# First batch's queries block by block; ten blocks' rows of x written later

## The chip, the cores and the metric

One NeuronCore of a Trainium2 chip runs the whole program. The metric is device time in microseconds. The kernel before takes 322.31 us, the median of 3 runs (322.21 to 324.1).

## What is computed

The reference has two parts. The first is attention without softmax, with a decay in place of it, for 8 batches of 8 heads, 576 positions and 64 channels, all in fp32:

```
scores = (1/8) * q @ k^T
ret    = scores * gamma_h ** (i - j)   where i >= j, else 0
x      = (ret @ v), heads side by side  -> 4608 rows of 512
```

The second sends each row of x to one of 8 experts: `logits = x @ w_gate`, the expert is the arg max, the gate its softmax probability, and `out = gate * (relu(x @ w1[e]) @ w2[e])` with matrices of 512x1024 and 1024x512.

## The kernel before, in words

**First half, about 170 us.** The work is tiled in 40 blocks: 8 batches (b) of 5 blocks (c), four of 128 positions and a rest of 64. Block number i is 5b + c. For each block the kernel loads k and v (256 KB each, in runs of 256 bytes, one for each head and position), scales k by the decay (`scale_k`), transposes it on TensorE (`put_TK`) and copies it out of PSUM on ScalarE (`get_TK`). Queries are scaled for a whole batch (`scale_q`, four pairs p of heads) and transposed (`put_TQ`, or `extra_TQ` through another bank). From batch 1 on, `load_q` gives a partition four neighbouring positions, so q moves in runs of 1 KB. `stage_SC` multiplies keys and queries and VectorE masks the product; `stage_AV` multiplies it with v; `stage_S` adds k^T v to a running state, `stage_se` copies that out, and `stage_IN` adds the state times the queries and copies the block's x, transposed, to SBUF. `stage_xb` casts it, `stage_R` turns it back into rows, and `put_rows` writes the rows to a DRAM buffer `x_rows` (128 KB a block). `stage_L1`, `stage_L2` and `route_batch` find each row's expert.

**Batch 0 before.** Its first 128 queries are a tile of their own (`qc0`, L155, scaled and transposed in `first_TQ`); the other 384 come as two loads in runs of 768 bytes (L161) and are scaled and transposed in four pairs (L854 to L862) ahead of `stage_AV(0)`.

**Order.** The order of work on every engine is written by hand. The loop at L917 does for iteration i: scale of k for block i+3, issue of the loads of k for i+9 and of v for i+7, transposes of i+2, `put_rows`, `stage_S(i+1)`, `stage_R(i-2)`, `stage_AV(i)`, `stage_SC(i+1)`, `stage_IN(i)`. Nearly all plain loads and all writes of rows are issued by SyncE (SP), one after the other, in program order; k and v have 7 buffers each, q two.

**Second half.** From block 34 on, the token lists of the experts are made, GpSimd gathers rows from `x_rows` (`gather`, L762) and TensorE runs the experts, with weights that GpSimd and SP load. The first gathers read the rows of batches 0 to 4 (blocks 0 to 24) and so wait for the writes of these.

TensorE is kept running in the first microseconds by transposes that nobody reads (`keep_busy`).

Of the kernel before, what the change touches and what calls it, by code (L numbers as in the profile page):

```python
# [19 lines left out]
P = 128  # L20
# [19 lines left out]
BA = 5  # L40
DW = DM // 2
# [4 lines left out]
def kernel(  # L46
# [48 lines left out]
    wk4 = p1.enter_context(tc.tile_pool(name="wk4", bufs=7))  # L95
    wk1 = p1.enter_context(tc.tile_pool(name="wk1", bufs=1))
# [68 lines left out]
    load_k(3)  # L165
    load_v(2)
    load_k(4)


# [129 lines left out]

# [11 lines left out]
    def put_TQ(ps, o, b, p):  # L311

        qq = qqs.pop((b, p))
        n, _, _ = spans(b)
        for s_ in range(n):
            for u in range(2):
                r = slice(u * DH, (u + 1) * DH)
                tr(ps[:, u, o + s_:o + n * DH:n], qq[r, s_, :], ident[r, r])
# [6 lines left out]
    def get_TQ(ps, o, b, p):  # L325

        n, _, t0 = spans(b)
        nc.scalar.copy(out=q_tile(b)[:, p, t0:512].rearrange("p (u t) -> p u t", u=2), in_=ps[:, :, o:o + n * DH])  # L328
# [8 lines left out]
    def first_TQ():  # L337

        qq = wk3.tile([P, H, DH], F32, tag="kk")
        nc.vector.tensor_tensor(out=qq[:, :, :], in0=qc0[:, :, :],  # L340
                                in1=qg[:, NCOL, :].unsqueeze(2).to_broadcast([P, H, DH]), op=ALU.mult)
        for p in range(NP):
            for u in range(2):
                r = slice(u * DH, (u + 1) * DH)
                tr(psx[:, u, p * DH:(p + 1) * DH],
                   qq[r, 2 * p:2 * p + 2, :].rearrange("p h d -> p (h d)"), ident[r, r])
        nc.scalar.copy(out=q_tile(0)[:, :, 0:P].rearrange("p a (u t) -> p u a t", u=2),  # L347
                       in_=psx[:, :, 0:256].rearrange("p u (a t) -> p u a t", t=DH))
# [10 lines left out]
    def get_TK(ps, o, i):  # L359
# [4 lines left out]
        kTs[i] = kT  # L364

# [134 lines left out]
    def stage_R(i):  # L500
# [17 lines left out]
        xr = wk4.tile([P, NP * P], BF16, tag="xr", name="xr")  # L518
# [6 lines left out]
        todo_x.append((x_rows[t0:t0 + m, 0:DW], xr[0:m, :].bitcast(F32)))  # L525

    todo_x = []
# [307 lines left out]
    def keep_busy(n):  # L835

        for a in range(n):
            tr(scr[:, a % 4 * P:(a % 4 + 1) * P], ident[:, :], ident[:, :])

# [352 lines left out]
```

## Time and profile before

| what | value |
|---|---|
| median of 3 runs | 322.31 us |
| the profiled execution's own time | 322.77 us |
| its span, first to last instruction | 321.0 us |
| TensorE matmul busy | 306.1 us, 95% |
| TensorE weight load busy | 229.3 us, 71% |
| ScalarE busy | 183.2 us, 57% |
| GpSimd busy | 187.0 us, 58% |
| VectorE busy | 150.4 us, 47% |
| moved by DMA | 71.04 MB, mean 221 GB/s |

A busy TensorE is not TensorE at its peak, since a matmul's end is modelled and overlaps the next one. DMA share is the time that packets took as a share of 16 engines; it can go over 1, as packets of one engine overlap. The rows of the trace are in the section below the change.

### The profile page before, as it was taken

How to read it: one execution, taken by the hardware profiler on the slowest of the kernel's cores; microseconds unless marked ns; L12 is line 12 of the kernel's file. 1: busy time of each engine (PE TensorE's matmuls, PEld its weight loads, DVE VectorE, ACT ScalarE, POOL GpSimd, SP SyncE). 2: the span in 40 equal slices, each digit the busy share in tenths (PEclk: the TensorE clock that was granted, in tenths of full speed). 3: DMA queues.
4: the chain of work that ended last, by engine and by line, in shares of the span. 5: the costliest groups of instructions: out<-in, count | busy, mean ns of one | idle time of the engine just before them, and what ended most of it. 6: DMA issues, size and time to landing. Idle time of an engine off the chain costs nothing. (4 is left out here: it accounts for less than half of the span.)

```text
span 321.0 us, 11816 instructions
## 1 busy us (share of the span) xinstructions
PE 306.1 (95%) x4965; PEld 229.3 (71%) x4965; DVE 150.4 (47%) x441; ACT 183.2 (57%) x371; POOL 187.0 (58%) x235
## 2 busy tenths in 40 slices
PE   6899999999999999899999999999999999999993
PEld 5688889888887887788875555677566665757562
DVE  4533366475574747557588321333333425242122
ACT  3568576786766768577576436444645353554530
POOL 4556665535463562445884577678877868564232
PEclk9999999999999999999999999999999999999999
DMA  8989999899999999984999996988999998973221
GB/s 176 233 186 247 200 231 234 214 235 231 237 247 205 257 227 239 242 201 103 204 202 247 212 251 196 254 312 225 286 270 338 249 286 261 305 272 112 77 99 53
DMA packets 114119, 71.04 MB, mean 221 GB/s; under 512 B 89438, under 2 KB 102238, under 8 KB 114064
## 3 DMA queue, kind: packets, MB, share of 16 engines
q1 hardware_dynamic: 102080, 43.84, 54.3%
q0 software_dynamic: 11456, 26.41, 34.0%
q8 instruction: 39, 0.64, 0.9%
q14 instruction: 16, 0.13, 0.1%
q10 hardware_dynamic: 528, 0.02, 0.1%
HBM read 67.31 MB, written 15.26 MB: 257 GB/s over the span
## 5 line engine op out<-in xcount | busy, mean ns | idle before, releaser
L830 ACT ACTIVATE ht<-pm 128x384 bf16<-128x384 f32 (+1 forms) x96 | 49.7, 518 | 54.0 <-PE pm L64 53.2
L304 POOL TENSOR_TENSOR kk<-kt,kg 128x512 f32<-128x512 f32 x39 | 40.9, 1050 | 57.4 <-PE pss L64 26.9
L64 PE MATMUL pm<-xt,w1b 128*128 128x384 bf16 (+1 forms) x512 | 71.1, 296 | 0.2
L64 PEld LDWEIGHTS <-w1b 128*128 128x128 bf16 x512 | 49.8, 98 | 20.0 <-DVE d L632 0.2
L1055 POOL DMA_INDIRECT out_dram<-ys,tids x40 | 42.9, 1073 | 34.8 <-DVE ys L1052 15.9
L429 DVE TENSOR_TENSOR sc<-pssc,mask 128x512 f32<-128x512 f32 x64 | 41.2, 686 | 24.7 <-PE pssc L64 23.9
L64 PEld LDWEIGHTS <-ht 128*128 128x128 bf16 (+1 forms) x328 | 32.5, 105 | 28.0
L762 POOL DMA_INDIRECT xg<-x_rows,tidg x40 | 42.2, 1054 | 14.5 <-issue 8.5
L64 PE MATMUL pss<-w2b,ht 128*128 128x512 bf16 (+2 forms) x168 | 38.8, 374 | 0.0
L64 PE MATMUL psx<-sc,vt 128*64 128x128 f32 (+1 forms) x640 | 38.2, 265 | 0.1
L294 POOL TENSOR_TENSOR qq<-qt,qg 128x512 f32<-128x512 f32 (+1 forms) x28 | 29.2, 1045 | 14.2 <-DMA qt<-in_q_dram 12.3
L64 PE MATMUL py<-w2b,ht 128*128 128x512 bf16 (+2 forms) x160 | 37.0, 374 | 0.0
L64 PE MATMUL pssc<-qT,kT 64*64 64x128 f32 (+2 forms) x896 | 35.5, 259 | 0.3 <-ACT qT L347 0.3
L1052 DVE TENSOR_SCALAR ys<-py,gsl 128x512 f32<-128x512 f32 (+2 forms) x20 | 14.7, 737 | 39.8 <-PE py L64 39.7
L474 ACT COPY xT<-psx 128x512 f32<-128x512 f32 x32 | 18.8, 586 | 25.4 <-PE psx L64 19.5
L811 ACT COPY xt<-pt 128x512 bf16<-128x512 bf16 (+1 forms) x38 | 21.3, 575 | 20.1 <-PE pt L67 19.5
L362 ACT COPY kT<-pst 128x512 f32<-128x512 f32 x40 | 23.6, 589 | 15.9 <-PE pst L67 14.9
L1052 DVE TENSOR_SCALAR ys<-pss,gsl 128x512 f32<-128x512 f32 (+2 forms) x21 | 15.5, 738 | 35.7 <-PE pss L64 34.6
L64 PEld LDWEIGHTS psx<-sc,vt 128*64 128x64 f32 (+1 forms) x640 | 30.6, 136 | 0.9 <-ACT qT L328 0.4
L64 PEld LDWEIGHTS pssc<-qT,kT 64*64 64x64 f32 (+1 forms) x896 | 28.1, 140 | 3.8 <-issue 0.8
L524 ACT COPY xr<-pssc 128x512 bf16<-128x512 bf16 (+1 forms) x37 | 21.9, 593 | 5.5 <-PE pssc L67 5.3
L64 PE MATMUL pss<-vt,kk 128*64 128x64 f32 x512 | 22.4, 227 | 2.6 <-issue 2.0
(141 smaller groups left out, 409.7 us busy)
## 6 DMA issues: line engine op xcount, KB each, us to landing
st<-in_moe_w_dram SPq DMA_DIRECT2D x20, 512.0 KB, 7.0
kt<-in_k_dram SPq DMA_DIRECT2D x32, 256.0 KB, 5.3
vt<-in_v_dram SPq DMA_DIRECT2D x32, 256.0 KB, 4.7
w1b<-in_moe_w_dram POOLq DMA_DIRECT2D x32, 256.0 KB, 6.0
qt<-in_q_dram SPq DMA_DIRECT2D x14, 512.0 KB, 5.4
x_rows<-xr SPq DMA_DIRECT2D x32, 128.0 KB, 4.2
w2b<-in_moe_w_dram POOLq DMA_DIRECT2D x12, 256.0 KB
kt<-in_q_dram SPq DMA_DIRECT2D x8, 128.0 KB, 5.9
```

What stands on the lines that cost most here:

```text
L64: nc.tensor.matmul(out=out, lhsT=lhsT, rhs=rhs, start=start, stop=stop, skip_group_check=True)
L294: eng.tensor_tensor(out=qq[:, 0:n, :].rearrange("p s (h d) -> p h s d", d=DH), in0=qts[b][:, h0:h0 + 2, 0:n, :], in1=qg[:, o:o + n, h0:h0 ...
L304: eng.tensor_tensor(out=kk[:, :, :], in0=kts.pop(i)[:, :, :], in1=kg[:, blocks[i][1], :].unsqueeze(2).to_broadcast([P, H, DH]), op=ALU.mult)
L362: mark["kT"] = nc.scalar.copy(out=kT[:, :, :].rearrange("p a (u t) -> p u a t", u=2), in_=ps[:, :, o:o + 256].rearrange("p u (a t) -> p u ...
L429: mark["sc"] = nc.vector.tensor_tensor(out=sc[:, j, :, :], in0=pssc[j][:, :].rearrange("p (a i) -> p a i", i=P), in1=mask[:, :].unsqueeze( ...
L474: mark["xT"] = nc.scalar.copy(out=xTs[b][:, c, :].rearrange("p (w t) -> p w t", w=2), in_=psx[:, :, 0:2 * P])
L524: nc.scalar.copy(out=xr_out, in_=ps)
L762: nc.gpsimd.indirect_dma_start(out=xg[0:m, :], out_offset=None, in_=x_rows[0:nr, :], in_offset=bass.IndirectOffsetOnAxis(ap=slots[ph][1][0 ...
L811: nc.scalar.copy(out=xts[(e, ph)][:, :, j * P:j * P + m], in_=pt[:, :, 0:m])
L830: mark["mm"] = nc.scalar.activation(out=ht[:, f0:f0 + per, :], in_=pm[:, :, :], func=AF.Relu)
L1052: nc.vector.tensor_scalar(out=ys[0:m, r], in0=py[0:m, r], scalar1=gsl[0:m, e, slots[ph][2] + j:slots[ph][2] + j + 1], scalar2=None, op0=AL ...
L1055: scatters.append(nc.gpsimd.indirect_dma_start(out=next(outs)[:, :], out_offset=bass.IndirectOffsetOnAxis(ap=slots[ph][0][0:m, e, j:j + 1] ...
```

## The change

Batch 0's queries are loaded as four blocks in the same form as k (256 KB, runs of 256 bytes), between the loads of k and v, scaled by VectorE block by block (`scale_qc`) and transposed with the block's keys (`first_T`). The blocks of batch 0 and the first of batch 1 get an order of their own, and the loop starts at i = 6. In it batch 1's queries are transposed at the end of batch 0, and batch 2's in blocks 2 to 4 of batch 1 and not in 1 to 4. The load of the gate weights `wgn` is issued after the first transposes' copies. Rows of blocks 0 to 9 go to ten buffers of their own (`wkr`, list `later`); from i = 16 on, every second iteration passes one of them to `put_rows`, which issues it in the iteration after. The transposes of `keep_busy` become bf16 matmuls on a zeroed tile.

```diff
+LATE = 10
+    wkr = p1.enter_context(tc.tile_pool(name="wkr", bufs=LATE))
...
-    qc0 = attc.tile([P, H, DH], F32, name="qc0")
-    load_k(0)
-    nc.sync.dma_start(out=qc0[:, :, :], in_=q[0, :, 0:P, :].rearrange("h p d -> p h d"))
-    load_k(1)
-    load_v(0)
+    fill = attc.tile([P, 512], BF16, name="fill")
+    nc.vector.memset(fill[:, :], 0.0)
+
+    def keep_busy(n, w=512):
+
+        for _ in range(n):
+            mm(scr[:, 0:w], fill[:, 0:P], fill[:, 0:w], True, True)
+
     qts[0] = ldq.tile([P, H, NCH, DH], F32, tag="q", name="qt")
-    for g in range(2):
-        hs = slice(g * NP, (g + 1) * NP)
-        nc.sync.dma_start(out=qts[0][:, hs, 0:NCH - 1, :],
-                          in_=q[0, hs, P:NCH * P, :].rearrange("h (p s) d -> p h s d", p=P))
-    load_k(2)
-    load_v(1)
-    load_k(3)
-    load_v(2)
-    load_k(4)
+    wgn = attc.tile([P, NPT, E], F32, name="wgn")
+    for c in range(NCH):
+        load_k(c)
+        nc.sync.dma_start(out=qts[0][:, :, c, :], in_=q[0, :, c * P:(c + 1) * P, :].rearrange("h p d -> p h d"))
+        if c > 0:
+            load_v(c - 1)
+    load_k(NCH)
+    load_v(NCH - 1)
+    load_q(1, 0)
+    load_v(NCH)
+    load_k(NCOL)
+    load_q(1, 1)
+    load_v(NCOL)
+    load_k(NCOL + 1)
+    load_v(NCOL + 1)
...
+    def scale_qc(c, eng=nc.gpsimd):
+        if c >= NCH:
+            return
+        qq = wkp.tile([P, NCH, P], F32, tag="qq")
+        eng.tensor_tensor(out=qq[:, :, :].rearrange("p a (h d) -> p (a h) d", d=DH), in0=qts[0][:, :, c, :],
+                          in1=qg[:, NCOL + c, :].unsqueeze(2).to_broadcast([P, H, DH]), op=ALU.mult)
+        qqs[c] = qq
...
+    def only_TQ(b, p):
+        ps = pair_banks()
+        put_TQ(ps, 0, b, p)
+        get_TQ(ps, 0, b, p)
...
+    def first_T(i, n=0):
+        ps = pair_banks()
+        put_TK(ps, 0, i)
+        if n:
+            get_TK(ps, 0, i)
+            keep_busy(n, 256)
+            ps = psx
+            put_TQc(ps, 0, i)
+            get_TQc(ps, 0, i)
+        else:
+            put_TQc(ps, 256, i)
+            get_TK(ps, 0, i)
+            get_TQc(ps, 256, i)
...
-        xr = wk4.tile([P, NP * P], BF16, tag="xr", name="xr")
+        xr = (wkr if i < LATE else wk4).tile([P, NP * P], BF16, tag="xr", name="xr")
...
-        todo_x.append((x_rows[t0:t0 + m, 0:DW], xr[0:m, :].bitcast(F32)))
+        (later if i < LATE else todo_x).append((x_rows[t0:t0 + m, 0:DW], xr[0:m, :].bitcast(F32)))
...
     scale_k(0, nc.vector)
-    stage_T(0, None, None)
-    keep_busy(2)
-    first_TQ()
     nc.vector.memset(psx[:, :, 256:512], 0.0)
+    scale_qc(0, nc.vector)
     nc.vector.memset(lt[:, P + DH:2 * P], 0.0)
     scale_k(1)
-    keep_busy(2)
+    scale_qc(1, nc.vector)
+    keep_busy(9)
+    first_T(0, 1)
+    nc.scalar.dma_start(out=wgn[:, :, :], in_=moe_w_gate.rearrange("(c p) e -> p c e", p=P))
+    keep_busy(3, 256)
     stage_SC(0)
...
+    load_k(NCOL + 2)
+    load_k(NCOL + 3)
+
+    def ahead(i):
+        load_v(i + 7)
+        load_k(i + 9)
+
+    for i in range(NCH):
+        if i == NCH - 1:
+            scale_q(1, 0)
+            scale_q(1, 1, nc.vector)
+            load_q(2, 1)
+        scale_k(i + 2)
+        scale_qc(i + 2, nc.vector)
+        if i == 1:
+            load_q(2, 0)
+        if i < NCH - 1:
+            first_T(i + 1)
+        else:
+            stage_T(i + 1, None, None)
+        put_rows()
+        stage_S(i)
+        stage_R(i - 2)
+        stage_se()
+        stage_xb(i - 1)
+        stage_AV(i)
+        stage_SC(i + 1)
+        stage_IN(i)
+        ahead(i)
+    only_TQ(1, 0)
+    extra_TQ(1, 1)
...
+    scale_q(1, 2)
+    scale_q(1, 3, nc.vector)
+    scale_k(NCOL + 1)
+    make_gate()
...
+    stage_T(NCOL, 1, 2)
+    todo_q.pop()()
+    extra_TQ(1, 3)
+    stage_SC(NCOL)
+    stage_xb(NCH - 1)
+    ahead(NCH)
...
+    stage_T(NCOL + 1, None, None)
+    put_rows()
+    stage_S(NCOL)
...
+    stage_AV(NCOL)
+    stage_L1(0)
+    stage_SC(NCOL + 1)
+    stage_IN(NCOL)
+    stage_S(NCOL + 1)
+    stage_se()
+    stage_T(NCOL + 2, None, None)
+    ahead(NCOL)
...
-        return [2 * c - 6, 2 * c - 5] if b == 0 and c > 2 else [c - 1] if b > 0 and c > 0 else []
+        return ([c - 2] + [c - 1] * (c == NCH) if c > 1 else []) if b == 1 else [c - 1] if c > 0 else []
...
-    for i, (b, c) in enumerate(blocks):
+    for i, (b, c) in list(enumerate(blocks))[NCOL + 1:]:
...
+        if i > 15 and i % 2 == 0:
+            todo_x.extend(later[:1])
+            del later[:1]
```

## Rows read from the trace of the kernel before

**Rows 1.** Stretches: from:to, its length, busy us of each engine, granted clock, DMA share, GB/s.
```profile
20.00:30.00 10.00, 9.04 (x236) 7.68 (x240) 3.71 (x7) 7.58 (x16) 5.99 (x11) 1.00 0.88 202
...
60.00:80.00 20.00, 19.88 (x530) 17.47 (x525) 12.09 (x38) 14.76 (x32) 9.49 (x10) 1.00 0.92 227
...
180.00:200.00 20.00, 20.00 (x126) 11.20 (x124) 4.14 (x10) 10.51 (x21) 13.52 (x16) 1.00 0.94 220
```

**Rows 2.** Timeline, VectorE: masks of blocks 0, 1, 5, 10 and 15 (start, length).
```profile
8.80 1.29 DVE L429 TENSOR_TENSOR sc<-pssc,mask 128x512 f32<-128x512 f32 x2 [0.53 <-PE pssc L64]
15.05 1.29 DVE L429 TENSOR_TENSOR sc<-pssc,mask 128x512 f32<-128x512 f32 x2 [2.79 <-PE pssc L64]
...
31.36 1.29 DVE L429 TENSOR_TENSOR sc<-pssc,mask 128x512 f32<-128x512 f32 x2 [0.22 <-PE pssc L64]
...
50.82 1.29 DVE L429 TENSOR_TENSOR sc<-pssc,mask 128x512 f32<-128x512 f32 x2 [0.21 <-PE pssc L64]
...
69.78 1.29 DVE L429 TENSOR_TENSOR sc<-pssc,mask 128x512 f32<-128x512 f32 x2 [0.22 <-PE pssc L64]
```

**Rows 3.** Timeline, TensorE: two waits, block 5's scores, pieces of a later block.
```profile
24.47 0.46 PE L67 MATMUL pst<-ident,qq 64*128 64x64 f32 x8 [0.96 <-POOL qq L294]
...
30.17 1.16 PE L64 MATMUL pssc<-qT,kT 64*128 64x128 f32 x16
...
36.83 0.69 PE L64 MATMUL pss<-vt,kk 128*64 128x64 f32 x16 [0.65 <-DMA vt<-in_v_dram]
...
110.30 1.08 PE L64 MATMUL pss<-xT,wgp 128*32 128x128 f32 x32
...
112.75 0.41 PE L67 MATMUL pst<-ident,qq 64*128 64x64 f32 x8
113.09 0.69 PE L64 MATMUL pss<-vt,kk 128*64 128x64 f32 x16
```

**Rows 4.** Stretches of 1 us, columns as in rows 1.
```profile
8.00:9.00 1.00, 1.00 (x26) 0.93 (x24) 0.46 (x3) 0.01 (x1) 0.25 (x1) 1.00 1.09 333
...
12.00:13.00 1.00, 0.83 (x14) 0.58 (x16) 0.26 (x1) 0.64 (x2) 0.94 (x1) 1.00 1.35 217
...
15.00:16.00 1.00, 0.99 (x24) 0.79 (x24) 0.95 (x2) 0.58 (x1) 0.44 (x1) 1.00 1.29 180
```

**Rows 5.** Timeline, scaling of queries: block 0, batch 1's first and second half.
```profile
5.48 0.69 DVE L340 TENSOR_TENSOR qq<-qc,qg 128x512 f32<-128x512 f32 x1 [0.85 <-DMA qc<-in_q_dram]
...
23.36 1.06 POOL L294 TENSOR_TENSOR qq<-qt,qg 128x512 f32<-128x512 f32 x1 [1.20 <-DMA qt<-in_q_dram]
...
26.28 1.06 POOL L294 TENSOR_TENSOR qq<-qt,qg 128x512 f32<-128x512 f32 x1 [0.41 <-DMA qt<-in_q_dram]
```

**Rows 6.** Writes of rows on SP: first, tenth, one late; all 40, issue to landing.
```profile
40.09 1.30 SPq L533 DMA_DIRECT2D x_rows<-xr  x1
...
74.04 0.92 SPq L533 DMA_DIRECT2D x_rows<-xr  x1
...
146.85 0.61 SPq L533 DMA_DIRECT2D x_rows<-xr  x1
...
DMA to landing us min/median/max: 2.3/4.3/13.6
```

**Rows 7.** First gather on GpSimd, its use on TensorE, gathers' time to landing.
```profile
150.83 1.13 POOL L762 DMA_INDIRECT xg<-x_rows,tidg  x1 [0.54 <-DVE tidg L746]
...
160.83 0.40 PE L67 MATMUL pss<-identb,xg 128*128 128x128 bf16 x4
...
DMA to landing us min/median/max: 2.8/5.6/10.6
```

**Rows 8.** TensorE's gaps with no releaser; the queue of instruction fetches.
```profile
128.49 0.50 PE L64 MATMUL pss<-vt,kk 128*64 128x64 f32 x9 [0.60 <-issue]
...
134.23 0.51 PE L64 MATMUL pss<-vt,kk 128*64 128x64 f32 x10 [0.97 <-issue]
...
q8 instruction: 39, 0.64, 0.9%
```

More of the change, by code (lines that the diff above doesn't have):

```diff
@@ L313, in put_TQ @@
         qq = qqs.pop((b, p))
-        n, _, _ = spans(b)
-        for s_ in range(n):
+        for s_ in range(NCH):
             for u in range(2):
                 r = slice(u * DH, (u + 1) * DH)
-                tr(ps[:, u, o + s_:o + n * DH:n], qq[r, s_, :], ident[r, r])
+                tr(ps[:, u, o + s_:o + NCH * DH:NCH], qq[r, s_, :], ident[r, r])
     def q_tile(b):
@@ L344, in first_TQ, with get_TQc @@
                 r = slice(u * DH, (u + 1) * DH)
[L345 to L348, printed above, removed]
+                tr(ps[:, u, o + p * DH:o + (p + 1) * DH], qq[r, p, :], ident[r, r])
+    def get_TQc(ps, o, c):
+        nc.scalar.copy(out=q_tile(0)[:, :, c * P:(c + 1) * P].rearrange("p a (u t) -> p u a t", u=2),
+                       in_=ps[:, :, o:o + 256].rearrange("p u (a t) -> p u a t", t=DH))
     def put_TK(ps, o, i):
@@ L524, in stage_R @@
             nc.scalar.copy(out=xr_out, in_=ps)
-        todo_x.append((x_rows[t0:t0 + m, 0:DW], xr[0:m, :].bitcast(F32)))
-    todo_x = []
+        (later if i < LATE else todo_x).append((x_rows[t0:t0 + m, 0:DW], xr[0:m, :].bitcast(F32)))
+    todo_x, later = [], []
     def put_rows():
@@ L832, in mm1 @@
         return ht
-    def keep_busy(n):
-        for a in range(n):
-            tr(scr[:, a % 4 * P:(a % 4 + 1) * P], ident[:, :], ident[:, :])
-    keep_busy(12)
     scale_k(0, nc.vector)
-    stage_T(0, None, None)
-    keep_busy(2)
-    first_TQ()
     nc.vector.memset(psx[:, :, 256:512], 0.0)
+    scale_qc(0, nc.vector)
     nc.vector.memset(lt[:, P + DH:2 * P], 0.0)
     scale_k(1)
-    keep_busy(2)
-    stage_SC(0)
-    stage_T(1, None, None)
-    stage_S(0)
-    stage_se()
-    keep_busy(3)
@@ L854 @@
-    for p in range(NP):
-        scale_q(0, p, nc.vector if p % 2 else nc.gpsimd)
-    scale_k(2)
-    for p in range(NP):
-        ps = psx if p % 2 == 0 else pair_banks()
-        put_TQ(ps, 0, 0, p)
-        get_TQ(ps, 0, 0, p)
-        if p == 1:
-            keep_busy(2)
-    stage_AV(0)
-    stage_IN(0)
-    stage_SC(1)
-    for i in range(5, 9):
-        load_v(i - 2)
-        load_k(i)
-        if i < 7:
-            load_q(1, i - 5)
+    scale_qc(1, nc.vector)
+    keep_busy(9)
+    first_T(0, 1)
@@ new lines @@
+    only_TQ(1, 0)
+    extra_TQ(1, 1)
+    constants = make_routing()
+    next(constants)
+    scale_q(1, 2)
[3 more added lines that the diff above has]
+    put_rows()
+    stage_S(NCH)
+    stage_R(NCH - 2)
+    stage_IN(NCH)
+    stage_T(NCOL, 1, 2)
[4 more added lines that the diff above has]
+    ahead(NCH)
+    next(constants)
+    scale_k(NCOL + 2)
+    load_q(3, 0)
+    stage_T(NCOL + 1, None, None)
+    put_rows()
+    stage_S(NCOL)
@@ L872, in pairs @@
+    stage_R(NCOL - 2)
+    stage_se()
+    stage_xb(NCH)
+    scale_k(NCOL + 3)
+    stage_AV(NCOL)
[6 more added lines that the diff above has]
+    ahead(NCOL)
     def pairs(b, c):
@@ L923 @@
         scale_k(i + 3)
-        if i == 1:
-            make_gate()
-        if i > 3:
-            next(constants, None)
+        next(constants, None)
         if b == B - 1 and c > 0:
@@ L960 @@
             stage_L2(b - 1)
-        for stage in ((stage_SC, stage_IN) if c < NCH else (stage_IN, stage_SC)) if i > 0 else ():
+        for stage in ((stage_SC, stage_IN) if c < NCH else (stage_IN, stage_SC)):
             stage(i + 1 if stage is stage_SC else i)
```

30 lines of the change are left out of this document (9 added, 21 removed).

## The prediction

> **What bounds the kernel now.** I read the stretches first. From 60 to 80 us TensorE is busy 19.88 of 20 us, from 180 to 200 us all 20; from 20 to 30 us it is busy 9.04 of 10 [rows 1]. So TensorE sets the pace of both halves, and only the start has holes. DMA is not far behind: its share is 0.88 to 0.94 in the same rows.
>
> The masks of VectorE then show the pace batch by batch [rows 2]. From block 10 to block 15, one steady batch, 69.78 - 50.82 = 18.96 us. Batch 1 takes 50.82 - 31.36 = 19.46 us, batch 0 31.36 - 8.80 = 22.56 us, and its first block alone 15.05 - 8.80 = 6.25 us. What can be won is here, before 31 us; batch 1 has 0.5 us over the steady pace, the rest has next to nothing that loads or writes of rows cause.
>
> TensorE's own waits say what the holes are [rows 3]: at 24.47 it has waited 0.96 us for scaled queries of batch 1, and at 36.83 it waits 0.65 us for a load of v (block 7). GpSimd, which scales those queries, waited in turn for their loads, 1.20 us before 23.36 and 0.41 before 26.28 [rows 5]. So the start is set in part by the chain of steps (queries of three blocks transposed in four rounds before block 0's products with v), in part by arrival of loads. SP issues them in program order and DMA moves them one behind the other, so I cost the start by bytes ahead of a load.
>
> **The change part by part.**
>
> *Block 0's path.* Now block 0 needs k0, q0 and v0 and no rounds of the other blocks' queries. But VectorE has `scale_qc(1)` queued ahead of block 0's mask: it waits for q1, the fourth load. In the kernel before, the second load's scaling starts at 5.48 [rows 5]; two more loads of 0.262 MB at 217 GB/s [rows 4] are 1.2 us each, so q1 lands near 7.9 and its 0.69 us end near 8.6, just before 8.80. Bounds 0 and +0.7 us for the mask; I take +0.3, as the early load rate is no better than that row. Block 1's mask then has q2 (0.69 us) ahead of it on VectorE. q2 is the seventh load, five after q0: 5.5 + 5 x 1.2 = 11.5, scaled by 12.2, so the mask comes near 12.8 and not 15.05: 2.2 us gained at that point.
>
> *Queries of batch 0 in runs of 256 bytes.* In the stretch from 8 to 9 us, where the 768-byte loads of batch 0's queries move, DMA gives 333 GB/s; from 12 to 13 us, with only k and v in runs of 256 bytes, 217 at an even higher share, 1.35 against 1.09; from 15 to 16 us 180 [rows 4]. So the three blocks, 0.786 MB, take 3.6 us and not 2.4: +1.3 us for everything behind them (at 180 GB/s +2.0; nothing if only bytes counted). The Trainium skill, "DMA: Bandwidth & Descriptors", section Specifications, wants at least 512 bytes a transfer for line rate, which speaks against this edit; the trace agrees with 333 against 217 GB/s. Were bytes all that counted, the sum below would be 1.3 us better.
>
> *Order of the loads.* The second half of batch 1's queries decides block 5, since its scores need all four pairs. Ahead of it one load of k (k6) is gone: -1.2 us; the runs give +1.3. So it lands where it did, 26.3 [rows 5]. From there: 1.06 us of scaling on GpSimd [rows 5], with k5 scaled before it, in its shadow, then two query transposes of 0.34 us each (113.09 - 112.75) [rows 3] and a copy that the second hides: block 5's scores start at 28.4 and not 30.17 [rows 3], **1.8 us earlier**. TensorE can keep that date: at the steady batch's pace, less 1.08 us for the logits [rows 3] and plus three query transposes of 0.34 us, batch 0 needs 18.9 us, 3.7 less than it took.
>
> Next the load of v for block 7. Before, it landed at 36.83 and TensorE waited for it [rows 3]. The change moves half of batch 2's queries (0.524 MB, at 333 GB/s 1.6 us) and k9 (1.2 us) behind it, against the 1.3 us of the runs: it lands near 35.3. TensorE would want it at 36.83 - 0.65 - 1.8 = 34.4, plus two products and transposes that now stand behind block 5's scores, 0.4 to 0.8 us: near 35. So about 0.3 us goes into a new wait, and the gain is 36.83 - 35.3 = **1.5 us**. The queries that were moved come 2.8 us after, near 38.1, and are scaled by 39.2; TensorE wants them near 38.8, as their transposes moved a block later too: 0 to 0.4 us, which the missing transpose of block 1 (0.34 us) pays.
>
> *Rows written late.* SP issues the first write of rows at 40.09 and the tenth at 74.04 [rows 6], so the loads up to there lose ten writes ahead of them (two are of half blocks). But by then TensorE waits for no load any more (batch 2 is at the steady pace) [rows 2]. The ten writes come back at one in two blocks from about 80 us to the last block row issue near 147. The cover is the loads' lead, and if that is gone each costs its place, 128 KB at 217 GB/s, 0.6 us. I take 0; bounds -0.5 us (batch 1's excess gone) and +1 us.
>
> *The rest, each at nothing.* The bf16 fillers end before k0's transposes are wanted, or stand at most 0.5 us in their way, hidden behind q0 at 5.5 us. The gate weights' load and preparation move to GpSimd's time after k6, and are wanted only by batch 0's logits. The extra 10 buffers of rows lengthen no step. The load of `wgn` waits on ScalarE for nothing that stands behind it.
>
> **The sum.** -1.5 us, from about block 8 to the end, as all that follows is paced by TensorE. Against the profiled execution's 322.77 (span 321.0 and 1.8 around it) that is 321.3; the execution lies 0.46 over the median of 322.31, so against the median **320.8 us**. What a measurement of this kernel can tell from no change is about 1%, 3.2 us: 319.1 to 325.5 is the same.
>
> **The rivals.**
>
> 1. *Loads hold nothing up; TensorE's pace alone sets batch 0.* For it: the sum of bytes is rough, DMA dips in the first 40 us (share 0.88) [rows 1] could be filled by the shorter lists of waits on SP, and without writes the lead grows. Against: [rows 3, 5] show the waits for loads. Then 3.7 us of batch 0 and 0.5 of batch 1 are won, a little more since batch 0 lacks the small routing products: 322.3 - 4.2 = 318.1.
> 2. *Gaps of instruction fetch go as well.* TensorE stands 0.60 and 0.97 us in the middle of a group of matmuls without any releaser, and a queue fetches instructions through the same engines [rows 8]. If a fuller DMA makes these, the lead won before 75 us takes them away: -1.5 - 1.6, 319.2, or 318.5 with part of the waits of rival 1. Against: two gaps in one execution are few.
> 3. *The gain is given back.* If the 256-byte loads run at 180 GB/s [rows 4] from the start, the 3.8 MB in such runs up to the second half of batch 1's queries take 3.6 us longer than at 217, or 1.8 if half of them do; block 5 is then at 30 to 31 and nothing is won: 322.3, up to 323.5.
> 4. *Slower: the first gather waits for a late write.* The last of the ten is issued near 147, like the late write of [rows 6], and the first gather, at 150.83, reads the rows of blocks 0 to 24 and so now waits for it. A gather lands in 5.6 us in the median [rows 7] and TensorE wants it at 160.83, so the write may land as late as 155.2, 8 us after its issue. The median is 4.3, the longest 13.6 [rows 6]. At 13.6 it lands at 160.6, the gather at 166.2, and TensorE stands 5.4 us: 320.8 + 5.4 = 326.2. Behind the gather on GpSimd stand the first experts' weight loads and the next gathers; these have more time. For it: the added wait is real. Against: DMA is at its slackest there, and 8 us are nearly twice the median.
> 5. *The edit does less than it says*, since the tenth write's turn or the order on VectorE undoes it: this falls into 3.
>
> **How the numbers follow.** My forecast, gains of 0.6 to 2.8 us: 0.45. Rival 1: 0.16. Rival 2: 0.10, both over 1% faster or at its edge. Rival 3 (with 5): 0.20. Rival 4: 0.09, most of it just over 1% slower. So faster 0.25, same 0.67, slower 0.08. The range goes from 317.2 (rival 1 with 1 us more for the routing products that batch 0 lacks) to 324.2 (rival 3 with the +1 us of the late writes, short of rival 4); the forecast's own range is 319.5 to 321.7.
>
> **What would show it.** After: block 1's mask near 12.8, block 5's near 29.6 and block 10's near 49.3; a load wait at block 7's state product below 0.7 us; 217 to 250 GB/s from 2 to 20 us with no stretch over 300; writes of rows on SP from about 62 us on (block 10's) and block 0's near 80; the first gather with no wait for a write. Wrong if block 5's mask comes before 28 (loads did not bind) or after 30.5 (they ran slower), if the gain at block 10 is not the gain at the end, or if TensorE waits for the first gathered rows.

## The result

The change makes the kernel slower: 328.23 us median (22 runs, 323.46 to 331.72) against 322.48 us for the kernel before beside it (22 runs), a ratio of 1.0121 [1.009, 1.0152], 3.9 us of 322.48. 320.8 us was forecast, and 324.2 us was the end of the range. The profiled execution took 331.49 us, span 329.7, so it is one of the longer ones. All ratios here are to the kernel before in the same job on the same chip and count undisturbed runs alone (none over 1.5% above the fastest of its kernel), while the medians take in all runs. The kernel before has medians of 322.5 to 330.2 us in the six jobs, over 2% apart, and 324.3, 329.5 and 330.2 us in three jobs on one chip; so the times of different jobs are not set against each other; the traces are, one execution each.

The masks of the changed kernel, the answer to [rows 2] (VectorE timeline; blocks 0, 1, 5, 10 and 15; line numbers are the changed file's, so L454 is the mask that was L429, L65 the matmul that was L64):

```profile
8.28 1.29 DVE L454 TENSOR_TENSOR sc<-pssc,mask 128x512 f32<-128x512 f32 x2
12.13 1.28 DVE L454 TENSOR_TENSOR sc<-pssc,mask 128x512 f32<-128x512 f32 x2
...
32.57 1.29 DVE L454 TENSOR_TENSOR sc<-pssc,mask 128x512 f32<-128x512 f32 x2 [4.41 <-PE pssc L65]
...
55.02 1.29 DVE L454 TENSOR_TENSOR sc<-pssc,mask 128x512 f32<-128x512 f32 x2 [0.26 <-PE pssc L65]
...
76.26 1.29 DVE L454 TENSOR_TENSOR sc<-pssc,mask 128x512 f32<-128x512 f32 x2 [1.48 <-PE pssc L65]
```

Block 1 is 2.9 us earlier than before, block 5 is 1.2 us later, block 10 is 4.2 us later, block 15 6.5. The last masks of the loop begin at 172.47 and 163.83 us, and from there to the end both take 157.2 us. So in these two executions the loss has two places, batch 1 (blocks 5 to 10: 22.45 us, was 19.46) and blocks 10 to 39 (117.45 us, was 113.01); the second half has none.

Stretches of the changed kernel, the answer to [rows 1] (columns as there):

```profile
20.00:30.00 10.00, 7.65 (x193) 6.42 (x186) 4.15 (x7) 5.50 (x12) 5.90 (x8) 0.91 0.92 215
30.00:40.00 10.00, 9.23 (x173) 8.10 (x171) 2.94 (x5) 4.97 (x11) 5.45 (x19) 0.75 0.99 194
60.00:80.00 20.00, 18.68 (x486) 16.29 (x487) 11.93 (x37) 13.62 (x29) 9.24 (x9) 1.00 0.88 197
180.00:200.00 20.00, 20.00 (x131) 11.13 (x130) 8.51 (x31) 10.15 (x21) 11.38 (x17) 1.00 1.17 229
```

From 20 to 30 us TensorE is busy 7.65 of 10 us (9.04 before), and the granted clock is 0.91 there and 0.75 in the next 10 us: it stood at half, the lower of its two levels, from 28.1 to 35.0 us. Before, it was full from 6.7 us to the end of the span's work. From 60 to 80 us TensorE lacks 1.3 us, with DMA slacker than before (197 GB/s, was 227).

What stands ahead of the half clock (TensorE timeline; block 5's key transposes, its queries, its scores; then the key transposes of blocks 7 and 8):

```profile
25.98 0.46 PE L68 MATMUL pst<-ident,kk 64*128 64x64 f32 x8
28.80 0.69 PE L68 MATMUL pst<-ident,qq 64*128 64x64 f32 x8 [2.35 <-POOL qq L294]
29.42 1.11 PE L68 MATMUL scr<-ident,qq 128*128 128x128 f32 x4
30.46 2.08 PE L65 MATMUL pssc<-qT,kT 64*128 64x128 f32 x16
...
38.32 0.46 PE L68 MATMUL pst<-ident,kk 64*128 64x64 f32 x8
39.56 0.47 PE L68 MATMUL pst<-ident,kk 64*128 64x64 f32 x8 [0.77 <-POOL csb L624]
```

and the scalings that TensorE waits for, the answer to [rows 5] (GpSimd and VectorE):

```profile
21.89 1.06 POOL L294 TENSOR_TENSOR qq<-qt,qg 128x512 f32<-128x512 f32 x1 [1.40 <-DMA qt<-in_q_dram]
22.07 1.42 DVE L294 TENSOR_TENSOR qq<-qt,qg 128x512 f32<-128x512 f32 x1
27.13 0.69 DVE L294 TENSOR_TENSOR qq<-qt,qg 128x512 f32<-128x512 f32 x1 [2.83 <-DMA qt<-in_q_dram]
27.15 1.59 POOL L294 TENSOR_TENSOR qq<-qt,qg 128x512 f32<-128x512 f32 x1 [2.25 <-DMA qt<-in_q_dram]
```

From 26.4 us TensorE has nothing that it may start, and it stands 2.35 us. The second half of batch 1's queries lands at 27.1, and both engines start on it at the same moment: GpSimd's scaling, the one that TensorE wants first, takes 1.59 us and not 1.06. Behind the gap the same four transposes of a pair take 1.11 us that take 0.66 at the full clock, and block 5's scores 2.08 (1.16 in [rows 3]). The last row is a wait that the kernel before does not have: the key transposes of blocks 7 and 8 now follow one another directly, and both go to the one pair of PSUM banks (`pst2`, one buffer), which ScalarE must first copy out. (The releaser named there is a wait that ended last by the profile; the run that moves these transposes apart, below, shows the cause.)

The largest stall further on (TensorE timeline, the scores of block 20, the first of batch 4):

```profile
94.28 1.16 PE L65 MATMUL pssc<-qT,kT 64*128 64x128 f32 x14
97.61 0.38 PE L65 MATMUL pssc<-qT,kT 64*128 64x128 f32 x2 [2.17 <-issue]
97.74 0.49 PE L68 MATMUL pst<-ident,kk 64*128 64x64 f32 x8
```

It has no releaser and falls in the middle of a group, like the two gaps of [rows 8]. If all of TensorE's instructions in the trace are counted in their order, such gaps fall where the count passes number 192 of a group of 256. One packet of the instruction queue [rows 8] seems to hold such a group: 39 packets of 16 KB go with 10,011 instructions of TensorE in the changed kernel, one for 257.

"Stalls" below are the steps of over 0.4 us at these marks, from the start of one instruction to the start of the next, added up (so each has the length of one instruction in it, and a few end with a wait that has a releaser). From 7 us to the end of the loop's blocks they come to 7.7 us, in the kernel before to 2.7; those that begin between 50 and 96 us to 5.0 and 0. TensorE's idle time with no releaser at the marks is less, 4.3 and 2.0 us, between 50 and 96 us 3.6 and 0, and the largest of these gaps runs past 96 us.

That these are late fetches shows in all traces together. They have 570 packets of the instruction queue between 7 us and the loop's last mask. Where a packet landed less than 1 us before TensorE came to the next mark, a stall followed in 88 of 93 cases; where it landed earlier, in 18 of 477.

```profile
50.00:96.00 46.00, 45.77 (x1197) 40.00 (x1196) 29.67 (x90) 33.05 (x71) 23.63 (x24) 1.00 0.95 229
```

```profile
50.00:96.00 46.00, 43.02 (x1110) 37.01 (x1100) 27.12 (x86) 31.51 (x67) 20.53 (x20) 1.00 0.95 214
```

The first row is the kernel before, the second the changed one: TensorE loses 2.75 us of this stretch at the full clock, with DMA equally busy; 2.0 us of it are idle time at the marks.

### The profile page after: what moved, and what is told of

Same layout as the page of the kernel before. It is cut to its first block, busy times and chain, and to the rows that moved or that the text cites. A ratio compares the mean times of both kernels' runs of the same rounds, so it can differ in the third digit from the quotient of the medians.

```text
span 329.7 us, 11796 instructions
## 1 busy us (share of the span) xinstructions
PE 309.6 (94%) x4957; PEld 230.2 (70%) x4957; DVE 151.9 (46%) x444; ACT 182.6 (55%) x370; POOL 184.6 (56%) x231
## 5 line engine op out<-in xcount | busy, mean ns | idle before, releaser
L65 PE MATMUL pm<-xt,w1b 128*128 128x384 bf16 (+1 forms) x512 | 71.1, 296 | 0.2
L65 PEld LDWEIGHTS <-w1b 128*128 128x128 bf16 x512 | 49.9, 98 | 20.0 <-DVE d L657 0.2
L454 DVE TENSOR_TENSOR sc<-pssc,mask 128x512 f32<-128x512 f32 x64 | 41.3, 686 | 27.2 <-PE pssc L65 27.0
L65 PEld LDWEIGHTS <-ht 128*128 128x128 bf16 (+1 forms) x328 | 32.5, 105 | 28.3 <-issue 0.4
L787 POOL DMA_INDIRECT xg<-x_rows,tidg x40 | 42.9, 1074 | 14.6 <-issue 7.6
L65 PE MATMUL pssc<-qT,kT 64*64 64x128 f32 (+2 forms) x896 | 37.5, 262 | 3.9 <-issue 3.6
L65 PE MATMUL psx<-sc,vt 128*64 128x128 f32 (+1 forms) x640 | 38.9, 267 | 0.3 <-issue 0.3
L65 PE MATMUL pss<-w2b,ht 128*128 128x512 bf16 (+2 forms) x168 | 38.8, 374 | 0.0
L65 PE MATMUL py<-w2b,ht 128*128 128x512 bf16 (+2 forms) x160 | 36.9, 374 | 0.1
L65 PEld LDWEIGHTS pssc<-qT,kT 64*64 64x64 f32 (+1 forms) x896 | 29.4, 143 | 8.3 <-issue 4.7
L499 ACT COPY xT<-psx 128x512 f32<-128x512 f32 x32 | 18.8, 587 | 26.0 <-PE psx L65 20.0
L836 ACT COPY xt<-pt 128x512 bf16<-128x512 bf16 (+1 forms) x38 | 21.3, 574 | 19.9 <-PE pt L68 19.3
L65 PEld LDWEIGHTS psx<-sc,vt 128*64 128x64 f32 (+1 forms) x640 | 31.3, 137 | 1.0 <-issue 0.4
L294 POOL TENSOR_TENSOR qq<-qt,qg 128x512 f32<-128x512 f32 x25 | 27.0, 1081 | 3.6 <-DMA qt<-in_q_dram 3.6
L65 PE MATMUL pss<-vt,kk 128*64 128x64 f32 x512 | 23.0, 230 | 1.6 <-issue 0.9
```

Source lines behind the costliest of these rows:

```text
L65: nc.tensor.matmul(out=out, lhsT=lhsT, rhs=rhs, start=start, stop=stop, skip_group_check=True)
L294: eng.tensor_tensor(out=qq[:, :, :].rearrange("p s (h d) -> p h s d", d=DH), in0=qts[b][:, h0:h0 + 2, :, :], in1=qg[:, 0:NCH, h0:h0 + 2].r ...
L454: mark["sc"] = nc.vector.tensor_tensor(out=sc[:, j, :, :], in0=pssc[j][:, :].rearrange("p (a i) -> p a i", i=P), in1=mask[:, :].unsqueeze( ...
L499: mark["xT"] = nc.scalar.copy(out=xTs[b][:, c, :].rearrange("p (w t) -> p w t", w=2), in_=psx[:, :, 0:2 * P])
L787: nc.gpsimd.indirect_dma_start(out=xg[0:m, :], out_offset=None, in_=x_rows[0:nr, :], in_offset=bass.IndirectOffsetOnAxis(ap=slots[ph][1][0 ...
L836: nc.scalar.copy(out=xts[(e, ph)][:, :, j * P:j * P + m], in_=pt[:, :, 0:m])
```

## The experiments

The table has nineteen profiles, one execution each: the start of block 5's and of block 10's mask, the time from block 10's to block 39's, the sum of the stalls that begin between 50 and 96 us (all in us), and the ratio of the timed runs to the kernel before. "Held" means that the first ten blocks' rows are written late; so they are in the changed kernel and in all its variants but e1, w1, x3 and z3.

| kernel | block 5 | block 10 | 10 to 39 | stalls | ratio |
|---|---|---|---|---|---|
| before | 31.36 | 50.82 | 113.0 | 0 | |
| before (b0) | 31.70 | 50.47 | 115.6 | 0 | |
| before (z4) | 31.64 | 51.07 | 112.6 | 0 | |
| w2, before, buffers only | 31.27 | 50.59 | 116.6 | 1.2 | 1.0005 [0.9948, 1.0062] |
| e2, before, held | 30.79 | 50.72 | 121.1 | 4.9 | 0.997 [0.9926, 1.0015] |
| y3, before, held, short lead | 31.96 | 53.10 | 116.5 | 3.6 | 1.0126 [1.0017, 1.0236] |
| changed | 32.57 | 55.02 | 117.5 | 5.0 | 1.0121 [1.009, 1.0152] |
| a0, changed again | 30.21 | 51.23 | 116.9 | 4.1 | 1.0101 [1.0035, 1.0166] |
| e3, fillers | 31.88 | 52.89 | 116.8 | 3.0 | 1.0116 [1.0044, 1.0187] |
| x1, rows twice | 32.61 | 56.33 | 118.8 | 4.4 | 1.0176 [1.0096, 1.0257] |
| x2, rows at the end | 31.20 | 53.95 | 118.0 | 4.6 | 1.0107 [1.0021, 1.0192] |
| y1, short lead | 30.32 | 54.58 | 114.5 | 1.3 | 1.0135 [0.9999, 1.0272] |
| y2, queries first | 32.67 | 55.13 | 116.4 | 5.4 | 1.0168 [1.0063, 1.0272] |
| z2, banks apart | 30.61 | 52.10 | 119.5 | 2.7 | 1.0135 [1.0048, 1.0223] |
| e1, rows at once | 31.18 | 55.24 | 112.5 | 0 | 1.0045 [1.0001, 1.009] |
| w1, buffers only | 29.50 | 50.51 | 115.2 | 1.6 | 1.018 [1.012, 1.024] |
| x3, at once, spaced | 29.94 | 56.75 | 117.8 | 4.2 | 1.0071 [1.0022, 1.0119] |
| z1, fewer bytes | 27.10 | 49.62 | 113.4 | 2.6 | 1.0019 [0.9969, 1.007] |
| z3, all mended | 27.12 | 48.77 | 112.5 | 1.7 | 0.9974 [0.9934, 1.0014] |

The first theory (A) was the gap for batch 1's queries and the half clock behind it; its rivals were instruction fetches that come late (B), for which the rows written late might be the reason, through their collisions with other transfers (C) or through their absence from the first 75 us (D), mere chance of single executions (E), and in the end the loads' lead, that is, how many blocks ahead of the masked one they are issued (F).

**a0: the changed kernel again**, unedited, in another job.

> The changed kernel once more, beside the others. Theory A (the clock): the wait of 2.35 us for the second half of batch 1's queries lowers the granted clock for some 7 us, so an execution with a drop after 28 us (mean clock under 0.993) is about 3.4 us longer than one without. Theory B (instruction fetch): TensorE's own instructions arrive later than before (packet of a fetch 3.1 us after the last boundary, 2.3 before), and its gaps at every 256th instruction add some 4 to 5 us; then executions without a clock drop are still 3 to 4 us over the kernel before.

1.0101: the loss is there again. But the gap for the second half of the queries is 0.59 us in the profiled execution, the clock does not fall there, and block 10 is at 51.23. So A cannot be all of it.

**e1: rows written at once** (without the ten buffers too, as `wkr` then has one).

```diff
-LATE = 10
+LATE = 0
```

> The changed kernel with rows of x written as before, none held back. If the late writes make the loss (rival C: they collide with loads and instruction fetches after 80 us), this is 3 to 5 us faster than the changed kernel. If the order of the first batch makes it (A and B), it stays within 1.5 us of the changed kernel, that is 3 to 6 us over the kernel before; if held-back rows did help, it is 1 to 2 us slower than the changed kernel.

**e2: the kernel before with the rows held back alone** (`wkr`, `later` and the two lines of the loop that pass rows on).

> The kernel before with the late rows alone: ten buffers, written one every second block from iteration 16 on. Rival C: 3 to 5 us slower than before. Theories A and B, if the new order of loads and of TensorE's first batch is what matters: within 1.5 us of before (320.5 to 324).

The new start without the held rows is at 1.0045, still not faster; the held rows without the new start are at 0.997, within the noise. Blocks 10 to 39 point the other way: 112.5 us in e1 without a stall between 50 and 96 us, 121.1 in e2.

**e3: fillers over the gap.**

```diff
+    keep_busy(11)
     stage_T(NCOL, 1, 2)
```

> The changed kernel with 11 filler matmuls (2.3 us) ahead of block 5's transposes, where TensorE waited 2.35 us for queries. Theory A: the granted clock stays full from 5 us to the end (mean 0.995 or more in all executions), batch 1 takes 2 to 3 us less, and the median falls by half of 3.4 to all of it, 1.7 to 3.4 us. Theory B alone: the clock stays full but the gaps at the instruction boundaries remain, and the time stays 3 to 4 us over the kernel before.

In the profiled execution the clock stayed full from 4.5 to 171.7 us, and its time lies within the others of this kernel; the ratio is 1.0116 all the same. The timed runs tell only their mean clock (0.990 to 0.996), not where it fell. A alone has fallen as far as one trace can show it.

**b0: the kernel before, a second profile, on the chip of the next runs.**

> The kernel before once more, for a second profile of it. Theory D (held-back rows let the loads run on alone; small reads at full rate delay TensorE's instruction fetches): between 50 and 96 us no gap at an instruction boundary, or under 0.7 us in all, and packets of 256 bytes take 18 to 19 ns in the mean from 50 to 75 us. If gaps there are chance (rival E), this profile has 2 us or more of them as likely as the changed kernel's.

Batch 1 takes 18.77 us there and nothing stalls between 50 and 96 us.

**x1: the missing writes put back** as writes of the same rows to a spare tile at the old time.

```diff
+        if i < LATE:
+            todo_x.append((spare[i * P:i * P + m, 0:DW], xr[0:m, :].bitcast(F32)))
```

> The changed kernel, which also writes the ten blocks' rows to an unused DRAM buffer at the time at which the kernel before writes them: 1.2 MB more traffic, the late writes as they were. Theory D: with writes between the loads again, the gaps at instruction boundaries from 50 to 96 us (2.5 to 5 us in the profiles with held-back rows) fall under 1 us and the time by 1 to 3 us against the changed kernel. Rival C (the late writes collide with loads): no gain, 0 to 1.5 us slower than the changed kernel.

**x2: the held rows all written from block 33 on.**

```diff
-        if i > 15 and i % 2 == 0:
-            todo_x.extend(later[:1])
-            del later[:1]
+        if i == NB - 8:
+            todo_x.extend(later)
+            del later[:]
```

> The changed kernel with all ten held-back rows written together at block 33, when loads are nearly done, and none from 80 to 140 us. Theory D: gaps from 50 to 96 us stay at 2.5 to 5 us and the time within 1.5 us of the changed kernel. Rival C: 1.5 to 3 us faster than it.

Stalls of 4.4 and 4.6 us remain, and the ratios stay at 1.0176 and 1.0107, so neither D (x1) nor C (x2) explains them.

**x3: rows at once, block 7's transposes earlier, batch 2's queries paired as before.**

```diff
+    stage_T(NCOL + 2, None, None)
     stage_IN(NCOL)
     stage_S(NCOL + 1)
     stage_se()
-    stage_T(NCOL + 2, None, None)
...
-        return ([c - 2] + [c - 1] * (c == NCH) if c > 1 else []) if b == 1 else [c - 1] if c > 0 else []
+        return [c - 1] if c > 0 else []
```

> The changed kernel with rows written at once, and two places of its order mended: block 7's transposes ahead of block 6's state, so that they and block 8's no longer follow each other through the one pair of PSUM banks (a gap of 0.8 to 0.9 us near 35 us in all profiles of the new order), and batch 2's queries one pair a block as before (a gap of 0.58 us at block 9). Theory: batch 1 takes 1.1 us less than with the rows-at-once version (21 us without clock drops), and the time is within 1 us of before; if these gaps are covered by later waits, it stays 1.5 us over before.

A mend that did harm: with the old pairing TensorE wants batch 2's queries before they are there, stands 3.75 us ahead of 39.48, and the clock falls to half from 37.6 to 44.4 us.

**y1 and y3: a short lead of the loads**, in the changed kernel and in e2's.

```diff
-        load_k(i + 9, mark.get("sc"))
+        if not 8 <= i <= 10:
+            load_k(i + (9 if i < 8 else 6), mark.get("sc"))
...
-        load_v(i + 7, mark.get("xT"))
+        if not 8 <= i <= 10:
+            load_v(i + (7 if i < 8 else 4), mark.get("xT"))
```

> The changed kernel, but from block 11 on a block's step loads k of six blocks ahead and v of four, not nine and seven (three steps load nothing in between), so that the loads' lead over the masked block stays at about 6, where it was in the kernel before, and not at 8. Theory F (the instruction fetches come late, and TensorE stands at every such place, because the loads run against the limit of their buffers): the sum of TensorE's stalls at the 256-instruction marks between 50 and 96 us falls from 4 to 5 us to below 1.5, the fetches' mean delay there from 3.4 us to about 2, and the run is 2 to 4 us below the changed kernel, ratio to the kernel before 0.998 to 1.005. Rival (the stalls belong to the new load on the engines, or to where the fetches fall, and not to the lead): stalls of 3 to 5 us remain and the ratio stays at 1.008 to 1.013. If the short lead starves the blocks, TensorE shows waits for kt or vt.

> The kernel before with the rows of the first ten blocks held back (as in the run with that part alone) and the lead of the loads kept short as in the run before this one. Theory F: the stalls between 50 and 96 us, 4.9 us with the rows held back alone, fall below 1.5, and the ratio to the kernel before comes to 0.985 to 0.994. Rival: stalls of 4 to 5 us and a ratio of 0.995 to 1.0, as without the cap.

The lead did fall to 5 or 6 blocks. The stalls came to 1.3 us in one and 3.6 in the other, and neither time fell: y3 is at 1.0126, the same kernel with the long lead (e2) at 0.997. F is not shown; at most a part is.

**y2: the second half of batch 1's queries loaded earlier.**

```diff
     load_q(1, 0)
+    load_q(1, 1)
     load_v(NCH)
     load_k(NCOL)
-    load_q(1, 1)
```

> The changed kernel, but the second half of batch 1's queries is loaded right behind the first half, ahead of v of block 4 and k of block 5, 2.4 us earlier. If the load order is what made TensorE stand 2.35 us for those queries, and the half clock from 28 us followed from that gap, then the wait ahead of block 5's scores is below 0.5 us, the clock stays full from 5 to 100 us in the profile, block 5's mask is at 29.5 to 30.5 and the run is 1.5 to 2.5 us below the changed kernel (ratio to the kernel before 1.003 to 1.007). If block 4's v or block 5's keys become the wait in their place, the same gap shows at block 4's product or block 5's transposes and the ratio stays at 1.01.

The one gap became several: 1.30 us at 22.04 and 0.71 at 27.71 for keys, 1.07 at 29.25 for queries, and block 5's mask stays at 32.67. So moving this one load forward gains nothing; what holds block 5 is the sum of the loads ahead of it, or the engines' own work. z1 tells these apart.

**z1: two loads of queries left out.** Blocks 1 and 2 use block 0's queries, so the output is another, and all work of the engines stays.

```diff
     for c in range(NCH):
         load_k(c)
-        nc.sync.dma_start(out=qts[0][:, :, c, :], ...
+        if c == 0:
+            nc.sync.dma_start(out=qts[0][:, :, c, :], ...
...
-        eng.tensor_tensor(..., in0=qts[0][:, :, c, :],
+        eng.tensor_tensor(..., in0=qts[0][:, :, 0, :],
```

> The changed kernel, but the queries of blocks 1 and 2 are not loaded (0.524 MB in runs of 256 bytes less); the queries of block 0 are used in their place, so the numbers are wrong and all the work of the engines stays. If the arrival of loads sets block 5 (the bytes ahead of batch 1's second half of queries), that half comes 2.4 us earlier (0.524 MB at 220 GB/s), the wait ahead of it, 0.6 to 2.35 us in the runs so far, goes, and block 5's mask comes at 28 to 29.5 (29.9 to 32.7 in all nine runs of the new order). If the engines' own work sets it, block 5's mask stays at 30 to 32. And if batch 1's excess is made by the loads too, blocks 5 to 10 fall from 21 to 27 us to about 20; if it is made by the new order of TensorE's work, they stay at 21 or more.

TensorE's timeline of z1 where the changed kernel has its gap:

```profile
24.20 0.46 PE L68 MATMUL pst<-ident,kk 64*128 64x64 f32 x8
24.51 0.41 PE L68 MATMUL pst<-ident,qq 64*128 64x64 f32 x8
24.88 0.66 PE L68 MATMUL scr<-ident,qq 128*128 128x128 f32 x4
25.60 1.47 PE L65 MATMUL pssc<-qT,kT 64*128 64x128 f32 x16
```

No wait: block 5's scores start at 25.60, its mask at 27.10, 2.4 to 5.6 us earlier than in the eleven profiles of the new order with all loads. So the arrival of loads binds block 5, and the ratio comes to 1.0019. (z2, of the same job, has all loads and is at 1.0135; the two intervals just overlap.) Batch 1 still takes 22.5 us, with the bank wait (0.77 us at 33.06) and two gaps at the fetch marks (0.41 and 0.91 us) in it.

**z2: the two transposes through the one pair of banks moved apart.**

```diff
     stage_SC(NCOL + 1)
+    stage_T(NCOL + 2, None, None)
     stage_IN(NCOL)
     stage_S(NCOL + 1)
     stage_se()
-    stage_T(NCOL + 2, None, None)
```

> The changed kernel, but block 7's key transposes stand right behind block 6's scores, ahead of block 5's and block 6's state products, so that they and block 8's no longer follow each other through the one pair of banks. The theory of the bank pair: the wait of 0.77 us, the same in eight profiles, is gone, and blocks 5 to 10 take 0.7 us less than otherwise; in the time that is a ratio about 0.002 lower than the changed kernel's, under what these rounds can tell. If the copy is only late for another reason, the wait moves to another place of the same two blocks.

TensorE's timeline of z2 at that place:

```profile
34.72 0.47 PE L68 MATMUL pst<-ident,kk 64*128 64x64 f32 x8
35.11 0.69 PE L65 MATMUL pss<-vt,kk 128*64 128x64 f32 x16
35.95 0.46 PE L68 MATMUL pst<-ident,kk 64*128 64x64 f32 x8 [0.16 <-ACT kT L373]
36.63 0.69 PE L65 MATMUL pss<-vt,kk 128*64 128x64 f32 x16 [0.21 <-ACT se L431]
```

0.77 us of waiting became 0.16 and 0.21 (ScalarE now has two copies close together): 0.4 us gained, not 0.7. The time cannot show that (1.0135).

**z3: both edits and rows at once.**

> Both edits above, and rows written at once: the new start with neither the late loads, nor the bank wait, nor the rows held back. If these three are what eats the start's 4 us, block 5's mask is at 28 to 29.5, block 10's at 48 to 49.5, the stalls at 256-instruction marks between 50 and 96 us below 1.5 us, and the ratio to the kernel before 0.988 to 0.996. If something else of the new order eats it (stalls of the instruction fetch in the denser start, the half clock behind them), block 10's mask stays at 51 or more and the ratio at 1.0 or above.

Masks of z3, blocks 0, 1, 5, 10 and 15:

```profile
8.69 1.29 DVE L455 TENSOR_TENSOR sc<-pssc,mask 128x512 f32<-128x512 f32 x2 [1.96 <-PE pssc L65]
11.77 1.29 DVE L455 TENSOR_TENSOR sc<-pssc,mask 128x512 f32<-128x512 f32 x2 [1.12 <-PE pssc L65]
...
27.12 1.29 DVE L455 TENSOR_TENSOR sc<-pssc,mask 128x512 f32<-128x512 f32 x2 [1.92 <-PE pssc L65]
...
48.77 1.29 DVE L455 TENSOR_TENSOR sc<-pssc,mask 128x512 f32<-128x512 f32 x2 [0.26 <-PE pssc L65]
...
69.32 1.29 DVE L455 TENSOR_TENSOR sc<-pssc,mask 128x512 f32<-128x512 f32 x2 [1.80 <-PE pssc L65]
```

Block 10 is 2.1 us ahead of the kernel before, and the ratio is 0.9974 [0.9934, 1.0014], against 1.0135 [1.0048, 1.0223] for z2 in the same job. The gain of 0.4 to 1.2% that was expected is not shown: in the trace one stall of 1.7 us takes most of the lead at block 15.

**z4: the kernel before, once more.**

> The kernel before, once more in profile on this chip. If batch 1's length is a property of the order, its blocks 5 to 10 take 18.8 to 19.9 us here too (19.46 and 18.77 in the two profiles so far; 21.0 to 26.8 in nine of the new order). If it is chance of single executions, some 21 us or more can show here as well.

Batch 1 takes 19.43 us. It takes 18.8 to 19.9 us in five of the six profiles of the old order (21.1 in y3) and 21.0 to 26.8 in the eleven of the new order with all loads, so its length is a property of the order.

**w1 and w2: the ten buffers, but rows written at once**, in the new and the old order.

```diff
-        (later if i < LATE else todo_x).append(
+        todo_x.append(
```

> The changed kernel with the ten extra buffers of rows, but each block's rows written at once. Stalls of TensorE at the 256-instruction marks between 50 and 96 us came to 1.3 to 5.4 us in all eleven profiles with rows held back and to 0, 0, 0, 0, 1.7 and 4.2 us in the six with rows written at once. If the lateness of the writes makes them, they fall below 1.7 us here, and the ratio to the kernel before is that of rows at once, 1.00 to 1.009. If it is the ten buffers (another place of all later buffers in SBUF), 2.5 to 5 us stay and the ratio is 1.008 to 1.016.

> The kernel before with the ten extra buffers of rows, rows written at once. Lateness: no stalls between 50 and 96 us (0 in three profiles of the kernel before), ratio 0.995 to 1.005. The buffers: 2.5 to 5 us of stalls, ratio 1.005 to 1.015.

Stalls of 1.6 and 1.2 us: by the traces it is the lateness more than the buffers. The times don't follow: w1 is at 1.018 [1.012, 1.024], no better than with rows held and worse than e1 (1.0045 [1.0001, 1.009]), which differs from it by the ten buffers alone but ran in another job. In the old order the same buffers cost nothing that shows (w2, 1.0005). So the times leave the buffers open as a cause.

No version here is shown to beat the kernel before; z3 leaves out loads that the kernel needs.

## Why the prediction was wrong

**Block 0's path: right.** Block 0's mask came at 8.28 (9.1 forecast), block 1's at 12.13 (12.8), and blocks 1 to 3 stay 2 to 3 us ahead.

**Runs of 256 bytes: borne out, but not tested alone.** Stretch from 2 to 20 us, before and after, and two short ones after:

```profile
2.00:20.00 18.00, 16.52 (x273) 13.34 (x275) 7.91 (x17) 8.17 (x18) 8.37 (x19) 1.00 1.20 233
```

```profile
2.00:20.00 18.00, 15.54 (x292) 11.46 (x294) 8.88 (x18) 8.53 (x19) 5.43 (x11) 1.00 1.19 216
...
8.00:9.00 1.00, 0.98 (x28) 0.85 (x26) 0.94 (x3) 0.22 (x1) 0.00 (x0) 1.00 1.37 204
...
15.00:16.00 1.00, 0.78 (x28) 0.54 (x18) 0.00 (x0) 0.14 (x1) 0.81 (x1) 1.00 0.63 127
```

At the same share of DMA 216 GB/s replace 233, and the stretch from 8 to 9 us that ran at 333 [rows 4] runs at 204. By 20 us that is 0.31 MB less, or 1.4 us at 217 GB/s, near the 1.3 us taken. But no run here changes the length of the runs alone, and part of it is not the runs: from 15 to 16 us the DMA engines of the changed kernel are not full (share 0.63, 127 GB/s). The rule of the Trainium skill that the prediction weighed, "DMA: Bandwidth & Descriptors", section Specifications (at least 512 bytes a transfer), speaks on the same side.

**Order of the loads: the step that failed first.** Forecast was "block 5's scores start at 28.4 and not 30.17". They started at 30.46. The landing was 0.85 us later than the 26.3 taken; the scaling took 1.59 us for the 1.06 taken from [rows 5], as both engines here start on the same load at once; and the half clock then stretched the transposes. That "TensorE can keep that date" was right (with two loads fewer, z1 takes 18.56 us from block 0's mask to block 5's; 18.9 was reckoned for batch 0), and it made the harm: an engine that comes earlier to the same late load stands longer, 2.35 us for the 0.96 in [rows 3]. z1 shows that the loads bind. Of the twelve timed runs of the changed kernel that the ratio counts, the three with a mean clock of 0.992 or less take 328.1 us in the mean and the nine others 325.5: 2.5 us go with the lower clock, which is no test of it. e3 shows that the loss stays without that fall. Over all profiles block 5 gains next to nothing: 31.15 us mean in eleven of the new order with all loads, 31.45 in six of the old.

**The products and transposes put behind block 5's scores: mis-sized.** I took 0.4 to 0.8 us, as a date for block 7 only. Block 6's transposes and block 5's state product are work that stands between the masks of blocks 5 and 10 and did not before (0.41 and 0.69 us busy in z1, at the full clock). This work is moved and not added, so a block 5 that comes no earlier than before is 1.1 us behind in work done. And the order there makes two waits on the pair of banks, 0.77 us at block 8's keys and 0.36 us at block 9 (for the last pair of batch 2's queries); I had named neither. With them come stalls at the fetches and half clock, which differ from one execution to the next (1.7 us at 47.5 and half clock from 48.0 to 51.4 in e1, none in a0). Block 10 is at 53.98 us in the mean of the eleven and at 51.13 in the six: 2.85 us lost, 0.9% of the time. In the times, e1 has the new start (loads and order) without the held rows at 1.0045.

**Rows written late: taken as 0 with bounds of -0.5 and +1.** In the traces it is more: the stalls between 50 and 96 us are 1.3 to 5.4 us in eleven profiles with rows held (mean 3.8) and 0 to 1.7 in seven of eight with rows at once (the eighth, x3, has 4.2); blocks 10 to 39 take 117.2 us against 114.5 in the mean. The timed runs do not separate it: 0.997 for it alone, and with the new start and all loads 1.0101 to 1.0176 held against 1.0045, 1.0071 and 1.018 at once. So its share of the 1.2% stays open: z1 (fewer loads, rows held) and e1 (all loads, rows at once) each come within 0.5% of the kernel before, and the two shares can't be told apart. What makes the fetches late stays open too: collisions (x2) and the missing writes (x1) are out, the buffers (w1, w2) by the traces and not by the times, and the loads' lead is neither shown nor excluded.

**The sum: "as all that follows is paced by TensorE".** This is the step that let a gain stand at the end. Rows of [rows 8] showed that TensorE also stands for its instructions; I made these a rival that could only gain ("two gaps in one execution are few") and did not ask whether the change could make more of them. The first traces have 7.7 us of such stalls up to the end of the loop's blocks, where the kernel before has 2.7; further traces have 5.4 (a0), and 3.5 and 2.2 (b0, z4). (The end of the range, 324.2 us, is not the sum that it is said to be either: rival 3's 322.3 to 323.5 us and 1 us more are 323.3 to 324.5. The measured time lies past both.)

**The rivals.** Nearest was the third, the gain given back, but the time (322.31 x 1.0121 = 326.2 us) went 2.7 us past its upper end, and for another reason: the loads ran at 216 GB/s from 2 to 20 us, not at 180. The fourth gives 326.2 us, the measured time, but by chance: it did not happen (GpSimd's first gather and its use on TensorE, the answer to [rows 7]):

```profile
159.47 1.12 POOL L787 DMA_INDIRECT xg<-x_rows,tidg  x1 [0.55 <-DVE tidg L771]
```

```profile
169.46 0.40 PE L68 MATMUL pss<-identb,xg 128*128 128x128 bf16 x4
```

10.0 us from issue to use, as before, and neither waited for a write. The first write of rows on SP came at 75.09 us, not near 62, as SP stood behind its loads; nothing waited for it.

Of my own signs, block 1's mask came true. The GB/s just missed: 216 from 2 to 20 us for the 217 to 250 named, with one stretch over 300 (303 GB/s from 19 to 20 us). Two of the signs named for being wrong came: block 5's mask after 30.5, and another difference at block 10 (4.2 us later) than at the end (span 8.7 us longer).

## What to carry to other kernels

Where an engine waits for a load, work taken away ahead of it only lengthens the wait; first ask which bytes must land by that date, and test it by leaving some out, as z1 did. An order written out by hand has to be walked through buffer by buffer: what moves behind a date meets its neighbours in a single-buffered bank. And with single executions that differ by 1 to 2%, a gain of 1.5 us needs both many timed runs and a trace that names the place.

## What the runs showed of the hardware

- TensorE stands at the change from one group of 256 instructions to the next when the fetch packet comes late (the 88 of 93 above). The packets took 0.9 to 2.6 us from start to landing, and the longest stall was 2.5 us. From a mark to the start of the next packet it took 1.3 to 1.8 us in the mean between 50 and 92 us in the three profiles of the kernel before, and 2.9 in the changed one. What delays the packets is not shown: over the 570 the delay goes only weakly with DMA's busy share or GB/s in the microsecond before (correlations of 0.21 and 0.29).
- During the gap of 2.35 us the granted clock went to half and stayed there for 6.8 us, though TensorE worked again from 28.8 us on. The fall at the gap of 3.75 us in x3 lasted 6.8 us as well, the others inside the traces 3.4.
- When VectorE and GpSimd start a scaling of 128x512 in f32 in the same 0.2 us, one of them takes 1.4 to 1.6 us for its 0.69 or 1.06 (17 pairs in these traces). In the 129 such scalings on GpSimd during which VectorE ran nothing it took 1.06 to 1.08 us.
